# Two forward passes of a four-layer attention kernel: scores in halves, sums in the score banks, one ring of PSUM banks, and a planner that looks further ahead

## The chip, the core and the metric

The kernel runs on one core of one Trainium2 chip. The metric is the device time of one execution in microseconds, median of several runs. The core's engines work side by side, each through its own list of instructions in order: TensorE (PE, matmuls, results into PSUM), VectorE (DVE), ScalarE (ACT), GpSimd (POOL) and SyncE (SP, which here issues nearly all DMAs). PSUM is eight banks of 512 floats in each of 128 partitions.

## The reference

Four residual layers over x (2048 tokens, 640 features, 32 heads of 20), A, B, A, B, with the same weights for both A and for both B; then the gradients of all five inputs for a given `grad_out`. The output is x after four layers and the gradients.

```python
# layer A: linear attention; phi(t) = where(t > 0, t + 1, exp(t)) + 1e-6
pq, pk = phi(q), phi(k)
kv = jnp.einsum("bhsd,bhse->bhde", pk, v)     # sums over all tokens
z = jnp.einsum("bhsd->bhd", pk)
o = jnp.einsum("bhqd,bhde->bhqe", pq, kv) / (jnp.einsum("bhqd,bhd->bhq", pq, z)[..., None] + 1e-6)

# layer B: causal attention over a window of 256 tokens
scores = jnp.einsum("bhqd,bhkd->bhqk", q, k) * (Dh ** -0.5)
p = _softmax(jnp.where(mask[None, None], scores, -1e9), axis=-1)
o = jnp.einsum("bhqk,bhkd->bhqd", p, v)

x = x + _A_ref(_layernorm(x), A_wqkv, A_wo)
x = x + _B_ref(_layernorm(x), B_wqkv, B_wo)   # and both once more
```

Layer A needs the sums kv and z over all tokens before its first output; layer B needs only the tile before and the two tiles ahead of it. That shapes the staging.

## The kernel before

Tokens are worked in 16 tiles of 128. `forward` has three stages. The first computes layer 0's q, k, v and its sums tile by tile (`a_first`, `kv_tile`). Then `ab_pass(0, False)` goes through the tiles once: the output of layer 0 (`a_num`, `out_proj`), layernorm, layer 1's qkv (`b_qkv`), its attention (`attn`), its output projection, and, one to three tiles behind, layer 2's layernorm, k and v (`a_first(items, l + 2, ...)`). `a_kv(2)` then forms layer 2's sums from all tiles, and `ab_pass(2, True)` does layers 2 and 3 and prepares what the backward part starts with (`dO`, `early`). `bwd_phase` follows; neither its functions nor its own planner's settings differ between the two kernels.

The order on every engine is made ahead of time. Each step calls `op(engine, duration, function, reads, writes)`; the items of a pass are sorted by a due time in tiles, and `Sched.order` places the operations one by one, with the assumed durations, on the engine that can start earliest. Among PE's operations it takes only those whose rank in the list is less than `ahead` (AHEAD = 12) past the first one not yet placed. `emit` writes the instructions in that order, and on the chip each engine follows it, waiting on semaphores. An operation on PE that waits therefore holds up all behind it.

PSUM in the passes: `R["mm"]` is a ring of three banks (`free=True`: the planner gives an operation the bank that comes free first) for all projections, transposes through PE and a_num; `R["s"]` is one tile of four banks for the scores; `R["pv"]` is one bank for the attention's values. Together eight.

The attention of a tile has eight groups of four heads. For a group, `scores` issues 4 matmuls for each key tile, 12 from the third tile on (L734: each uses 32 of PE's 128 rows, at row offset 32 x head, and head `hh` writes bank `hh` of the score tile), then one exp on ACT over all four banks (L739), and the masks: `affine_select` on POOL (L743, twice) and, for three key tiles, one multiply on DVE (L748) and one more select on POOL (L751). `values` multiplies the exps with v in two halves of two heads (L768); 16 heads share a values bank, which is then emptied by a reciprocal and a multiply on DVE (L775, L776). The multiply writes the tile `oB`; in the second pass oB lies in the memory of the tile `kv`, and the trace calls it kv there. The exps lie in a ring of three tiles `e_sb`.

`a_kv` sums with one bank of the ring for each of five bands of features: 16 matmuls each over the tiles (L571), and a sixth bank for z: 80 matmuls of one column (L583). DVE multiplies each band with a mask into `mbd` (L590, `masked`), as soon as that band is summed, and spreads z into `zsel` (L595, L597, `store_mbd`); SP stores `mbd`. `kv_tile`, used in the first stage alone, instead adds one tile's ten matmuls (five bands, five columns of z) to two banks `sums` that stay open for all tiles. `a_num` reads mbd (L647 numerators; the 32-column matmuls of L480 with zsel are the denominators). A projection is a chunk of 320 columns: five matmuls at L480, emptied by one operation of DVE or ACT.

Of the kernel before, what the change touches and what calls it, by code (L numbers as in the profile page):

```python
# [23 lines left out]
QL = 3  # L24
QS = 0.5


# [59 lines left out]
class Sched:  # L87

    def __init__(self, tc, ahead=None, lead=None):
        self.tc, self.ops, self.lw, self.rd, self.ahead, self.lead = tc, [], {}, {}, ahead, lead

# [32 lines left out]
    def order(self):  # L126
# [42 lines left out]
        while len(out) < len(self.ops):  # L169
# [35 lines left out]
            o.start = t  # L205
# [24 lines left out]
class Kern:  # L230
# [130 lines left out]
    def forward(self):  # L361
# [7 lines left out]
        with ExitStack() as st:  # L369
# [90 lines left out]
            def vp(n):  # L460
                return 150 + 1.04 * n
# [101 lines left out]

            def a_kv(l):
                def band_sum(m, lo, hi):
                    w_ = hi - lo
                    ps = R["mm"].buf()
                    for t0 in range(0, TT, 4):
                        def f(t0=t0):
                            for tt in range(t0, t0 + 4):  # L570
                                nc.tensor.matmul(ps.t[:, 0:w_], lhsT=pk(tt, m * P, (m + 1) * P), rhs=vv(tt, lo, hi),  # L571
                                                 start=(tt == 0), stop=(tt == TT - 1))
                        op("PE", pe([w_] * 4), f, [k for tt in range(t0, t0 + 4) for k in
                                                   (("pk", tt, 2), ("pk", tt, 3), ("vv", tt, 4), ("vv", tt, 5))], [ps])
                    masked(m, ps, 0)

                for m in range(DT):
                    band_sum(m, *self.band[m])
                zp = R["mm"].buf()
                for m in range(DT):  # L580
                    def f(m=m):
                        for tt in range(TT):
                            nc.tensor.matmul(zp.t[:, m:m + 1], lhsT=pk(tt, m * P, (m + 1) * P),  # L583
                                             rhs=self.ones_bf[:, 0:1], start=(tt == 0), stop=(tt == TT - 1))
                    op("PE", pe([1] * TT), f, [("pk", tt, i) for tt in range(TT) for i in (2, 3)], [zp])
                store_mbd(l, zp, 0)

            def masked(m, ps, off):
                lo, hi = self.band[m]
                op("DVE", vp(hi - lo), lambda: nc.vector.tensor_mul(  # L590
                    mbd[:, m, lo:hi], ps.t[:, off:off + hi - lo], self.bmask[:, m, 0:hi - lo]), [ps, "masks", "zeros"],
                   [("mbd", m)])

            def store_mbd(l, zp, off):
                op("DVE", vp(DT), lambda: nc.vector.tensor_copy(zcol, zp.t[:, off:off + DT]), [zp], ["zcol"])  # L595
                for m in range(DT):
                    op("DVE", v2(H), lambda m=m: nc.vector.tensor_scalar(  # L597
                        out=zsel[:, m, :], in0=self.hmask[:, m, :], scalar1=zcol[:, m:m + 1], scalar2=None,
                        op0=ALU.mult), ["zcol", "masks", "zeros"], [("zsel", m)])
                dma("SP", lambda: self.sv[l]["mbd"].rearrange("(m p) e -> p m e", p=P), lambda: mbd, 960 * KB,  # L600
                    [(k, m) for m in range(DT) for k in ("mbd", "zsel")], [])

            def kv_tile(tt, sums):

                def f():
                    for m, (lo, hi) in enumerate(self.band):
                        i, off = at_[m]
                        lhsT = pk(tt, m * P, (m + 1) * P)
                        nc.tensor.matmul(sums[i].t[:, off:off + hi - lo], lhsT=lhsT, rhs=vv(tt, lo, hi),
                                         start=(tt == 0 and m == 0), stop=(tt == TT - 1), skip_group_check=True)  # L610
                        nc.tensor.matmul(sums[1].t[:, zoff + m:zoff + m + 1], lhsT=lhsT, rhs=self.ones_bf[:, 0:1],
                                         start=(tt == 0 and m == 0), stop=(tt == TT - 1), skip_group_check=True)
# [102 lines left out]
            def attn(l, b, qT, kTs, vts, oT, out):  # L715
# [10 lines left out]
                def scores(g):  # L726
                    def f():
                        s = R["s"].buf()

                        def mm_s():  # L730
                            for j in range(nkt):
                                for hh in range(4):
                                    r = slice(HPAD * hh, HPAD * (hh + 1))
                                    nc.tensor.matmul(s.t[:, hh, j * P:(j + 1) * P], lhsT=kTs[j].t[r, g, :],  # L734
                                                     rhs=qT.t[r, g, :], start=True, stop=True,
                                                     tile_position=(HPAD * hh, 0))
                        op("PE", 210 + 55 * nkt, mm_s, [qT] + kTs, [s])
                        e = es[g] = R["e"].buf()
                        op("ACT", av(4 * nkt * P), lambda: nc.scalar.activation(  # L739
                            e.t[:, :, 0:nkt, :], s.t[:, :, 0:nkt * P].rearrange("p h (i q) -> p h i q", q=P),  # L740
                            ACT.Exp, scale=self.c_att), [s], [(e, p_, j) for p_ in (0, 1) for j in range(nkt)])
                        for p_ in (0, 1):
# [13 lines left out]
                def values(g, p_):  # L756
                    def f():
                        e = es[g]
                        q = 4 * g // 16
                        if q not in pvs:  # L760
                            pvs[q] = R["pv"].buf()
                        pv = pvs[q]

                        def mm_pv():
                            for hh in (2 * p_, 2 * p_ + 1):
                                h = 4 * g + hh
                                for j in range(nkt):
                                    nc.tensor.matmul(pv.t[:, h % 16, :], lhsT=e.t[:, hh, j, :],  # L768
                                                     rhs=vts[j].t[:, h, :], start=(j == 0), stop=(j == nkt - 1))
                        op("PE", pe([DH + 1] * 2 * nkt), mm_pv,  # L770
                           [(e, p_, j) for j in range(nkt)] + [(v, c) for v in vts for c in (4, 5)], [pv])
                        if g % 4 == 3 and p_ == 1:
                            h0 = 16 * q
                            li = lambda: lv.t[:, i_, h0:h0 + 16]
                            op("DVE", 200, lambda: nc.vector.reciprocal(li(), pv.t[:, :, DH]), [pv], [(lv, i_, q)])  # L775
                            op("DVE", vp(16 * DH), lambda: nc.vector.tensor_tensor(  # L776
                                out=o.t[:, h0 * DH:(h0 + 16) * DH].rearrange("p (h d) -> p h d", d=DH),
                                in0=pv.t[:, :, 0:DH], in1=li().unsqueeze(2).to_broadcast([P, 16, DH]), op=ALU.mult),
                               [pv, (lv, i_, q)], [(o, q)] + ok)
# [145 lines left out]
            def ab_pass(l, last):  # L925
# [81 lines left out]
                else:  # L1007
                    a_first(items, l + 2, 2.09, -0.2)
                run(items)

# [9 lines left out]
            sums_p = pool1("sums_ps", **PS)  # L1020
            sums = [Ring(1, tiles=[sums_p.tile([P, 512], F32, name=f"sums{i}")], name="sums").buf() for i in range(2)]
            items = []
# [8 lines left out]
            run(items)  # L1031
            for m in range(DT):
                masked(m, sums[at_[m][0]], at_[m][1])
            store_mbd(0, sums[1], zoff)
            S.emit()
# [753 lines left out]
```

## Time and profile before

| what | value |
|---|---|
| median of three runs | 2114.66 us (2114.49 to 2114.9) |
| the profiled execution: its own time | 2109.33 us |
| its span, first to last instruction | 2107.4 us |
| granted TensorE clock, mean | 0.984 |
| first A layer | 0 to 76 us |
| first pass | 76 to about 400 us, last exp of scores ends at 387.26 |
| second pass | 407 to 706 us, last exp of scores ends at 700.5 |
| backward part | 706 to 2107 us |

How to read it: the page gives busy time of each engine as a share of the span, and the costliest groups of instructions with line, engine, operation, tiles and shapes. A window row gives, for each engine, busy us and (instructions), then the granted clock (1.00 is full), the share of the DMA engines and GB/s. A timeline row is start, duration, engine, line, operation, tiles, shapes, count; in brackets is the engine's idle time just before and what ended it. A row of waits is: who waited, for whose result, us in total, how many times, the longest. Durations of matmuls include a modelled tail, so two in a row overlap in the rows; start to start tells their cost.

### The profile page before, as it was taken

The page shows a single profiled execution, that of the slowest core. Times are in us where ns is not written, and L with a number is a line of the kernel's source. Part 1 is how long each engine was busy: PE and PEld are TensorE (multiplying, and loading weights), DVE is VectorE, ACT ScalarE, POOL GpSimd, SP SyncE. Part 2 cuts the span into 40 slices and gives each one's busy share as a digit, 9 for nine tenths or more (in the row PEclk, how much of TensorE's full clock was granted, in tenths as well). Part 3 has the DMA queues.
Part 4 walks back from the last instruction along what each step waited for, and adds up shares of the span by engine and source line. Part 5 has one row for each costly group of instructions (what it writes and reads, how often), then busy time and mean ns, then how long its engine had stood idle before and what let it go on. Part 6 is the DMA issues. An engine that isn't in the chain of part 4 may idle for free. (4 is left out here: it accounts for less than half of the span.)

```text
span 2107.4 us, 68065 instructions
## 1 busy us (share of the span) xinstructions
PE 1982.7 (94%) x28001; PEld 1362.9 (65%) x28001; DVE 1437.3 (68%) x2978; ACT 1169.3 (55%) x1946; POOL 840.8 (40%) x1851
## 2 busy tenths in 40 slices
PE   7889999799898899999999999999999999999999
PEld 5656555566555577777665677656777776666764
DVE  8767776567776799999143369606999994444641
ACT  5367888358777688887222223215888872211330
POOL 1044555236666666665022213203666652221210
PEclk9999999899999899999999999998999999999999
DMA  8689877379998699997999999738889879899973
GB/s 309 196 189 216 180 180 184 109 175 195 211 202 191 129 151 165 159 156 122 190 200 191 256 209 207 181 97 159 139 144 144 147 122 183 190 204 241 212 172 90
DMA packets 926568, 373.72 MB, mean 177 GB/s; under 512 B 816944, under 2 KB 902960, under 8 KB 926000
## 3 DMA queue, kind: packets, MB, share of 16 engines
q1 hardware_dynamic: 885616, 337.77, 79.3%
q10 hardware_dynamic: 40640, 31.60, 5.2%
q8 instruction: 219, 3.59, 0.7%
q14 instruction: 93, 0.76, 0.1%
HBM read 106.73 MB, written 112.23 MB: 104 GB/s over the span
## 5 line engine op out<-in xcount | busy, mean ns | idle before, releaser
L1606 DVE SCALAR_TENSOR_TENSOR ds_sb<-pair,e_sb 128x768 bf16<-128x768 f32 x480 | 439.4, 952 | 18.8 <-POOL e_sb L1595 6.8
L1591 ACT ACTIVATE e_sb<-pair 128x768 bf16<-128x768 f32 x480 | 379.1, 812 | 96.1 <-PE pair L1571 94.8
L739 ACT ACTIVATE e_sb<-s_ps 128x1536 bf16<-128x1536 f32 (+2 forms) x256 | 350.6, 1370 | 98.7 <-PE s_ps L734 56.6
L743 POOL TENSOR_SCALAR_AFFINE_SELECT e_sb<-e_sb 128x256 bf16<-128x256 bf16 x512 | 213.2, 439 | 378.2 <-ACT e_sb L739 361.0
L1098 PEld LDWEIGHTS <-om 128*128 128x128 bf16 x1920 | 188.3, 98 | 157.0 <-DMA om<-o 2.2
L1098 PE MATMUL mm_ps<-wq,dqT 128*128 128x320 bf16 x1920 | 276.0, 299 | 4.7 <-ACT dqkv L1430 3.7
L1259 POOL TENSOR_TENSOR gw<-w,gcar 128x640 f32<-128x640 f32 x64 | 89.9, 1405 | 456.7 <-ACT w L1256 451.2
L1098 PE MATMUL mm_ps<-dqkv,om 128*128 128x480 bf16 x1280 | 268.9, 367 | 1.4 <-DMA om<-hn 1.4
L1598 POOL TENSOR_SCALAR_AFFINE_SELECT e_sb<-e_sb 128x256 bf16<-128x256 bf16 x448 | 182.1, 406 | 199.9 <-ACT e_sb L1591 199.9
L1595 POOL TENSOR_SCALAR_AFFINE_SELECT e_sb<-e_sb 128x256 bf16<-128x256 bf16 x512 | 206.5, 407 | 78.5 <-ACT e_sb L1591 78.5
L1098 PEld LDWEIGHTS <-dqT 128*128 128x128 bf16 x1920 | 185.9, 98 | 79.0 <-issue 6.6
L1241 ACT ACTIVATE dh<-mm_ps 128x320 f32<-128x320 f32 x128 | 56.0, 437 | 292.0 <-PE mm_ps L1098 234.3
L1624 PE MATMUL dsT_ps<-ident,ds_sb 128*128 128x128 bf16 x2244 | 189.5, 221 | 3.8 <-DVE dsT L1627 1.3
L480 PE MATMUL mm_ps<-Wqkv_B,hnTB 128*128 128x320 bf16 x960 | 180.4, 300 | 10.7 <-DMA hnTB<-hnB 6.5
L768 PEld LDWEIGHTS <-e_sb 128*128 128x128 bf16 x2880 | 122.2, 97 | 74.7 <-POOL e_sb L751 20.0
L768 PE MATMUL pv_ps<-v_slab,e_sb 128*128 128x32 bf16 x2880 | 145.0, 178 | 19.0 <-DVE oB L776 4.6
L1627 DVE COPY dsT<-dsT_ps 128x768 bf16<-128x768 bf16 x268 | 147.8, 552 | 7.7 <-PE dsT_ps L1624 4.7
L480 PE MATMUL mm_ps<-Wqkv_A,pqT 128*128 128x320 bf16 x780 | 139.2, 302 | 5.8 <-DVE oA L657 2.4
L1571 PE MATMUL pair<-VTg,dOTg 32*128 32x384 bf16 (+2 forms) x896 | 139.9, 318 | 1.0 <-ACT e_sb L1591 0.3
L1624 PEld LDWEIGHTS <-ds_sb 128*128 128x128 bf16 x2244 | 132.4, 98 | 12.1 <-issue 9.3
L1645 PE MATMUL dqvk_ps<-Qsl,ds_sb 128*128 128x32 bf16 x2880 | 134.7, 177 | 3.2 <-ACT dqkv L1627 2.7
L1261 DVE SCALAR_TENSOR_TENSOR gcar<-hn,sm,gw 128x640 bf16<-128x640 bf16 x64 | 80.4, 1256 | 82.0 <-POOL gw L1259 82.0
(178 smaller groups left out, 3556.5 us busy)
## 6 DMA issues: line engine op xcount, KB each, us to landing
qkvp<-qk_slab SPq DMA_DIRECT2D x32, 512.0 KB, 3.1
om<-o SPq DMA_DIRECT2D x20, 512.0 KB, 5.9
hn<-hn SPq DMA_DIRECT2D x64, 160.0 KB, 3.0
om<-hn SPq DMA_DIRECT2D x20, 512.0 KB, 4.9
ee<-e SPq DMA_DIRECT2D x32, 320.0 KB, 3.7
e<-ee SPq DMA_DIRECT2D x52, 160.0 KB, 2.0
qkvp<-v_slab SPq DMA_DIRECT2D x32, 256.0 KB, 2.7
o<-o SPq DMA_DIRECT2D x48, 160.0 KB, 3.4
```

The costliest lines, as they stand in the source:

```text
L480: nc.tensor.matmul(ps.t[:, w0:w0 + width], lhsT=lhsT(), rhs=rhs(), start=start, stop=stop)
L739: op("ACT", av(4 * nkt * P), lambda: nc.scalar.activation(e.t[:, :, 0:nkt, :], s.t[:, :, 0:nkt * P].rearrange("p h (i q) -> p h i q", q=P) ...
L743: op("POOL", 440, lambda p_=p_: nc.gpsimd.affine_select(out=e.t[:, 2 * p_:2 * p_ + 2, nkt - 1, :], in_=e.t[:, 2 * p_:2 * p_ + 2, nkt - 1, ...
L768: nc.tensor.matmul(pv.t[:, h % 16, :], lhsT=e.t[:, hh, j, :], rhs=vts[j].t[:, h, :], start=(j == 0), stop=(j == nkt - 1))
L1098: nc.tensor.matmul(ps.t[:, w0:w0 + width], lhsT=lhsT(), rhs=rhs(), start=start, stop=stop)
L1571: nc.tensor.matmul(ps[:, i, c0:c0 + len(ks) * P], lhsT=ld[g][lhs][r, q * P:(q + 1) * P], rhs=ld[g][rhs][r, ks[0] * P:(ks[-1] + 1) * P], st ...
L1591: nc.scalar.activation(e, PR[h][:, :, 0:3 * P].rearrange("p i (j q) -> p i j q", q=P), ACT.Exp, scale=self.c_att)
L1595: nc.gpsimd.affine_select(out=e[:, :, j, :], in_=e[:, :, j, :], compare_op=ALU.is_ge, fill=0.0, base=0, pattern=[[0, 2], [-1, P]], channel ...
L1598: nc.gpsimd.affine_select(out=e[:, :, j, :], in_=e[:, :, j, :], compare_op=ALU.is_ge, fill=0.0, base=-1, pattern=[[0, 2], [1, P]], channel ...
L1606: nc.vector.scalar_tensor_tensor(out=DS[n][:, hs], in0=PR[h][:, :, 0:3 * P].rearrange("p i (j q) -> p i j q", q=P), scalar=self.c_att, in1 ...
L1624: nc.tensor.transpose(ps[:, i, j, :], DS[n][:, 2 * p + i, j, :], self.ident)
L1627: (nc.vector.tensor_copy if eng == "DVE" else nc.scalar.copy)(out, in_)
```

## The change

Four parts, all in `forward` and in the planner:

- The scores of the last 12 groups of each pass (tile 14 from group 4 on, and tile 15) are done in two halves of two heads: six matmuls and one exp over two banks each, with keys of their own, `("s_ps", 0)` and `("s_ps", 1)`. All other groups stay whole. The planner's duration for a half's matmuls is that of a whole group.
- `a_kv` and `masked` go. In the first pass 16 operations `kv_tile` add layer 2's sums to banks 2 and 3 of the score tile; the first takes them over after the last scores' exp. `store_mbd` does the five masked products, then z.
- The three `mm` banks and the values bank become one ring of four, and a tile's values take a bank of it.
- In the planner of the passes an operation of ACT, DVE or POOL frees its engine 100, 80 or 50 ns ahead of its result, and PE's window is 16 operations instead of 12. The first stage keeps 12 and no such lead.

```diff
+TAIL = dict(PE=0, ACT=100, DVE=80, POOL=50)
...
-                free[e] = t + o.dur
-                o.end = free[e] + (170 if e == "PE" else 0)
+                free[e] = t + o.dur - (self.tail[e] if self.tail else 0)
+                o.end = t + o.dur + (170 if e == "PE" else 0)
...
-            def a_kv(l):
-                def band_sum(m, lo, hi):
...
-            def masked(m, ps, off):
...
+            def store_mbd(l, sums, keys=()):
+                for m, (lo, hi) in enumerate(self.band):
+                    i, off = at_[m]
+                    op("DVE", vp(hi - lo), lambda m=m, lo=lo, hi=hi, i=i, off=off: nc.vector.tensor_mul(
+                        mbd[:, m, lo:hi], sums[i][:, off:off + hi - lo], self.bmask[:, m, 0:hi - lo]),
+                       ["sums", "masks", "zeros"] + list(keys), [("mbd", m)])
+                op("DVE", vp(DT), lambda: nc.vector.tensor_copy(zcol, sums[1][:, zoff:zoff + DT]), ["sums"] + list(keys), ["zcol"])
...
-            def kv_tile(tt, sums):
+            def kv_tile(tt, sums, keys=None):
...
-                   [("pk", tt, 2), ("pk", tt, 3), ("vv", tt, 4), ("vv", tt, 5)], sums)
+                   [("pk", tt, 2), ("pk", tt, 3), ("vv", tt, 4), ("vv", tt, 5)], ["sums"] if tt else ["sums"] + (keys or []))
...
                 def scores(g):
                     def f():
-                        s = R["s"].buf()
...
-                        op("PE", 210 + 55 * nkt, mm_s, [qT] + kTs, [s])
                         e = es[g] = R["e"].buf()
-                        op("ACT", av(4 * nkt * P), lambda: nc.scalar.activation(
-                            e.t[:, :, 0:nkt, :], s.t[:, :, 0:nkt * P].rearrange("p h (i q) -> p h i q", q=P),
-                            ACT.Exp, scale=self.c_att), [s], [(e, p_, j) for p_ in (0, 1) for j in range(nkt)])
+                        for h0, h1 in ((0, 2), (2, 4)) if 2 * b * G + 2 * g >= (2 * TT - 3) * G else ((0, 4),):
+                            halves = range(h0 // 2, h1 // 2)
+
+                            def mm_s(h0=h0, h1=h1):
+                                for j in range(nkt):
+                                    for hh in range(h0, h1):
...
+                            op("PE", 210 + 55 * nkt, mm_s, [qT] + kTs, [("s_ps", p_) for p_ in halves])
+                            op("ACT", av((h1 - h0) * nkt * P), exp, [("s_ps", p_) for p_ in halves],
+                               [(e, p_, j) for p_ in halves for j in range(nkt)])
...
-                            pvs[q] = R["pv"].buf()
+                            pvs[q] = R["mm"].buf()
...
                     a_first(items, l + 2, 2.09, -0.2)
+                    for tt in range(TT):
+                        items.append((max(16.1 + 0.15 * tt, tt + 3.9), len(items), lambda tt=tt: kv_tile(
+                            tt, [s_ps[:, i, :] for i in (2, 3)], [("s_ps", 1)])))
...
-            S = Sched(tc, ahead=AHEAD)
-            R["mm"] = banks(pool("mm_ps", **PS), 3, "mm_ps")
-            R["s"] = Ring(1, tiles=[pool("s_ps", **PS).tile([P, 4, 512], F32, name="s_ps")])
-            R["pv"] = ring("pv_ps", 1, [P, 16, 32], F32, **PS)
+            S = Sched(tc, ahead=16, tail=TAIL)
+            R["mm"] = banks(pool("mm_ps", **PS), 4, "mm_ps")
+            s_ps = pool("s_ps", **PS).tile([P, 4, 512], F32, name="s_ps")
             ab_pass(0, False)
-            a_kv(2)
+            store_mbd(2, [s_ps[:, i, :] for i in (2, 3)], [("s_ps", 1)])
             ab_pass(2, True)
```

More of the change, by code (lines that the diff above doesn't have):

```diff
@@ L87, with __init__ @@
 class Sched:
-    def __init__(self, tc, ahead=None, lead=None):
-        self.tc, self.ops, self.lw, self.rd, self.ahead, self.lead = tc, [], {}, {}, ahead, lead
+    def __init__(self, tc, ahead=None, lead=None, tail=None):
+        self.tc, self.ops, self.lw, self.rd, self.ahead, self.lead, self.tail = tc, [], {}, {}, ahead, lead, tail
     def op(self, eng, dur, fn, r=(), w=(), dma=None, prio=None):
@@ L562, in a_qkv @@
                 return [chunk(ci) for ci in cis]
-            def a_kv(l):
-                def band_sum(m, lo, hi):
[L566 to L586, printed above, removed]
@@ L588, in masked @@
-            def masked(m, ps, off):
[L589 to L595, printed above, removed]
+            def store_mbd(l, sums, keys=()):
[5 more added lines that the diff above has]
+                op("DVE", vp(DT), lambda: nc.vector.tensor_copy(zcol, sums[1][:, zoff:zoff + DT]), ["sums"] + list(keys), ["zcol"])
@@ L727, in f @@
                     def f():
-                        s = R["s"].buf()
[L730 to L736, printed above, removed]
@@ L737, in f, with exp @@
-                        op("PE", 210 + 55 * nkt, mm_s, [qT] + kTs, [s])
-                        e = es[g] = R["e"].buf()
-                        op("ACT", av(4 * nkt * P), lambda: nc.scalar.activation(
-                            e.t[:, :, 0:nkt, :], s.t[:, :, 0:nkt * P].rearrange("p h (i q) -> p h i q", q=P),
-                            ACT.Exp, scale=self.c_att), [s], [(e, p_, j) for p_ in (0, 1) for j in range(nkt)])
+                        e = es[g] = R["e"].buf()
+                        for h0, h1 in ((0, 2), (2, 4)) if 2 * b * G + 2 * g >= (2 * TT - 3) * G else ((0, 4),):
[3 more added lines that the diff above has]
+                                    for hh in range(h0, h1):
+                                        r = slice(HPAD * hh, HPAD * (hh + 1))
+                                        nc.tensor.matmul(s_ps[:, hh, j * P:(j + 1) * P], lhsT=kTs[j].t[r, g, :],
+                                                         rhs=qT.t[r, g, :], start=True, stop=True,
+                                                         tile_position=(HPAD * hh, 0))
+                            def exp(h0=h0, h1=h1):
+                                nc.scalar.activation(
+                                    e.t[:, h0:h1, 0:nkt, :],
+                                    s_ps[:, h0:h1, 0:nkt * P].rearrange("p h (i q) -> p h i q", q=P),
+                                    ACT.Exp, scale=self.c_att)
+                            op("PE", 210 + 55 * nkt, mm_s, [qT] + kTs, [("s_ps", p_) for p_ in halves])
+                            op("ACT", av((h1 - h0) * nkt * P), exp, [("s_ps", p_) for p_ in halves],
+                               [(e, p_, j) for p_ in halves for j in range(nkt)])
@@ L767, in mm_pv @@
                                 for j in range(nkt):
-                                    nc.tensor.matmul(pv.t[:, h % 16, :], lhsT=e.t[:, hh, j, :],
+                                    nc.tensor.matmul(pv_h()[:, h % 16, :], lhsT=e.t[:, hh, j, :],
                                                      rhs=vts[j].t[:, h, :], start=(j == 0), stop=(j == nkt - 1))
@@ L774, in f @@
                             li = lambda: lv.t[:, i_, h0:h0 + 16]
[L775 removed]
+                            op("DVE", 200, lambda: nc.vector.reciprocal(li(), pv_h()[:, :, DH]), [pv], [(lv, i_, q)])
                             op("DVE", vp(16 * DH), lambda: nc.vector.tensor_tensor(
                                 out=o.t[:, h0 * DH:(h0 + 16) * DH].rearrange("p (h d) -> p h d", d=DH),
[L778 removed]
+                                in0=pv_h()[:, :, 0:DH], in1=li().unsqueeze(2).to_broadcast([P, 16, DH]), op=ALU.mult),
                                [pv, (lv, i_, q)], [(o, q)] + ok)
@@ L1020, in forward @@
             sums_p = pool1("sums_ps", **PS)
-            sums = [Ring(1, tiles=[sums_p.tile([P, 512], F32, name=f"sums{i}")], name="sums").buf() for i in range(2)]
+            sums = [sums_p.tile([P, 512], F32, name=f"sums{i}") for i in range(2)]
             items = []
@@ L1031, in forward @@
             run(items)
-            for m in range(DT):
-                masked(m, sums[at_[m][0]], at_[m][1])
-            store_mbd(0, sums[1], zoff)
+            store_mbd(0, sums)
             S.emit()
```

5 lines of the change are left out of this document (3 added, 2 removed).

## The prediction, made before the changed kernel had run

> **What bounds the kernel now.** First the page's header and its table of busy times, for the total and the fullest engine:
>
> ```profile
> span 2107.4 us, 68065 instructions
> PE 1982.7 (94%) x28001; PEld 1362.9 (65%) x28001; DVE 1437.3 (68%) x2978; ACT 1169.3 (55%) x1946; POOL 840.8 (40%) x1851
> ```
>
> PE is the bound, but an average over 2107 us hides where it idles. So next the busy times in windows cut at the stages: start, ramp of the first pass, its steady part, its last 12 groups of scores, the turn to the second pass, the same again, then the backward part.
>
> ```profile
> core 0: us, PE busy (x) PEld busy (x) DVE busy (x) ACT busy (x) POOL busy (x), PEclk, DMA share, GB/s
> 100.00:362.00 262.00, 242.00 (x3831) 154.83 (x3830) 189.47 (x527) 203.46 (x275) 132.61 (x329) 1.00 0.83 191
> 362.00:387.30 25.30, 20.97 (x358) 13.93 (x357) 13.62 (x39) 19.65 (x21) 14.64 (x36) 0.87 0.30 96
> 387.30:430.00 42.70, 32.84 (x363) 23.58 (x362) 25.81 (x73) 6.43 (x19) 1.17 (x3) 0.88 0.50 145
> 430.00:676.50 246.50, 226.35 (x3723) 147.09 (x3723) 179.97 (x482) 186.79 (x215) 149.40 (x342) 1.00 0.92 194
> 676.50:706.30 29.80, 22.43 (x378) 14.92 (x377) 16.66 (x41) 17.69 (x13) 18.78 (x42) 0.89 0.44 115
> ```
>
> The change can only move these 606 us and the ramp ahead of them (76 to 100): PE's instruction lists of the two kernels agree before row 1259 and after row 18782, that is, in the first A layer and in all of the backward part (1401 us, PE 97% busy). PE idles 20 us in each steady part, 4.3 and 7.4 in the two tails, 9.9 in the turn. What ends those idles is in the waits of PE over 76 to 706 us:
>
> ```profile
> PE s_ps L734 <- ACT e_sb L739: 9.0, 26, 0.7
> PE pv_ps L768 <- DVE oB L776: 4.6, 10, 0.8
> PE mm_ps L480 <- DVE pp L548: 4.3, 16, 0.8
> PE pv_ps L768 <- DVE kv L776: 4.1, 5, 0.9
> PE mm_ps L480 <- DVE oA L657: 2.4, 8, 0.4
> PE mm_ps L480 <- DVE qk_slab L699: 2.3, 7, 0.3
> PE mm_ps L480 <- DVE gcar L548: 1.1, 1, 1.1
> ```
>
> (us in total, times, longest.) The first is the score banks, not yet emptied by the exp. The two L776 rows are the one values bank, not yet emptied by the multiply into oB (8.7 us). In the others PE waits on DVE for tiles that none of these matmuls reads directly (pp reaches PE only through a DMA): a bank of the ring of three (10.1 us, and single rows of 0.6).
>
> **Halves.** The timeline of the first tail shows the loop:
>
> ```profile
> 370.31 0.35 PE L734 MATMUL s_ps<-QT,KT 32*128 32x128 bf16 x12 [0.71 <-ACT e_sb L739]
> 370.59 0.58 PE L480 MATMUL mm_ps<-Wqkv_A,pqT 128*128 128x320 bf16 x3
> 370.75 1.45 ACT L739 ACTIVATE e_sb<-s_ps 128x1536 bf16<-128x1536 f32 x1 [0.50 <-POOL e_sb L743]
> 372.25 0.35 PE L734 MATMUL s_ps<-QT,KT 32*128 32x128 bf16 x12 [0.39 <-ACT e_sb L739]
> ```
>
> Scores, 0.35; hand-over, 0.09; exp, 1.45; hand-over, 0.05: 1.94 us from score to score, and nothing shortens it while one tile of four banks is written and read as a whole. The last 12 groups take 25.2 us in pass one (362.02 to the end of the exp at 387.26) and 24.0 in pass two (676.53 to 700.5). In halves, PE fills two banks while ACT reads the other two. ACT's cost: one more instruction per group. The backward part has an exp of just that size, 768 columns:
>
> ```profile
> 721.43 1.51 ACT L1591 ACTIVATE e_sb<-pair 128x768 bf16<-128x768 f32 x2 [0.22 <-PE pair L1571]
> ```
>
> Two in a row take 1.51, against 1.45 for the whole: 0.06 a group. ACT's floor is then 12 x 1.51 = 18.1 us, plus in pass one the other ACT work among these groups (six of 0.42, one rs pair of 0.49: 3.0). So at best -4.1 (25.2 to 21.1) and -5.9 (24.0 to 18.1). PE's cost: row 370.59 follows 0.28 after the scores begin, so a group occupies PE for 0.28: twelve matmuls of 128 columns in the time of five transposes of 128 columns (396.10 to 396.39), because its four heads lie in four row groups and run side by side. A half has two side by side, and costs between half of the 0.28 (no loss) and all of it (+0.28 a group, 3.3 us a pass). By a four-matmul group (429.76, the next matmul at 429.93: 0.17) most is fixed cost, so I take the whole +0.28. Pass one then has 21.0 + 3.3 = 24.3 of PE work in 25.2, part of it at half clock (its row 378.68 takes 0.98 for what row 370.59 did in 0.58). I take -2.0 a pass, -4.0. Worst: if PE sets the pace and nothing hides the second half, +3.3 a pass. Masks keep pace: POOL has about 1.28 a group (two of 0.44, one of 0.40).
>
> The Trainium skill, TensorEngine Tiling (Array Packing), Tiling Modes, says that a change of tiling mode drains TensorE, which speaks against twice as many score blocks. The 0.17 for four matmuls against 0.28 for twelve, 0.014 each, leaves some 0.115 a block, which agrees; by that rule 24 more blocks cost 2.8 us of PE, and if none were hidden the -4.0 would be -1.2.
>
> **Sums in the score banks.** Removed: a_kv's sums, after the pass.
>
> ```profile
> 400.68 0.65 PE L571 MATMUL mm_ps<-gcar 128*128 128x140 bf16 x8
> 406.95 0.42 PE L647 MATMUL mm_ps<-mbd,pqT 128*128 128x320 bf16 x3
> 407.62 0.73 PE L480 MATMUL mm_ps<-mbd,pqT 128*128 128x32 bf16 x5 [0.25 <-DVE mbd L597]
> 75.44 1.17 DVE L590 TENSOR_TENSOR mbd<-sums,bmask 128x140 bf16<-128x140 f32 x5 [0.39 <-PE sums L609]
> ```
>
> They fill PE from 400.68 to 406.95 (12 of the matmuls came earlier, at 396.39), and the first denominator starts at 407.62. Added: the same 160 matmuls as 16 tiles of ten, 0.44 us each (first A layer: 27.24 to 27.68). In the new list two tiles stand right after the last scores, 13 more among what was there, the sixteenth just ahead of the second pass. PE's idles from the last exp (387.26) to 400.68 are 0.79 + 0.44 + 0.45 + 1.36 + 0.65 = 3.7; 0.75 more comes free at 396.39. Fifteen tiles are 6.6: 2.2 overflow onto the path. That path is long and serial (last values, oB, out-projection, layernorm, qkv of the last tile). The last v copy ends at 401.37; then 0.05, the sixteenth tile 0.44, then DVE's five masked products, zcol and zsel, which no longer lie beside the sums: in the first layer the first denominator (77.00) starts 1.6 after the last sum. 401.37 + 0.5 + 1.6 + 2.2 = 405.7 against 407.62: -1.9. Ends: -4.1 (no overflow), +2.5 (all 6.6 on the path). The first tile waits for the last exp with all of PE's queue behind it; next there are the last values, which wait for that exp and then 0.8 of POOL's masks, so the wait is free; uncovered, the two tiles cost 0.9. The store of mbd stays one DMA on SP, behind the same products. The second pass's scores wait for the products to leave these banks, some 20 us before they are due.
>
> **One ring of four.** Along the two instruction lists, with 0.136 us a 320-column matmul (20 in 2.71 at 69.85) and 0.026 a values matmul, I counted the PE work between two uses of a bank: under 0.9 us 23 times before and 11 after, under 1.2 us 70 and 27; after a values block it is never under 1.1. Emptying a values bank took 1.2 (block ends 380.52, next at 381.73). So the 8.7 us should go, and half of the 10.1. Of these 13.8 I let half arrive: in the steady parts scores follow each other by 2.0 to 2.2, against the loop's 1.94, and PE is 92% busy. -6.9; ends -13.8 and 0. At the start of pass two both out-projection chunks shared a bank (414.07 waits 0.58 for x L676); now they have two: -0.6.
>
> **Planner.** Tails and 16 instead of 12 add no instruction; they reorder. The other waits on DMA (hnTB 6.5, oTA 4.5) and on masks (e_sb 4.4 + 3.8 + 1.3) are 20 us; a third either way is 7. I take 0. Clock: 0.87 to 0.89 over 98 us is about 23 us at half speed, in which matmuls took 1.7 times as long; up to 9.6 us if PE-bound throughout. I take no change.
>
> Sum: -4.0 - 1.9 - 6.9 - 0.6 = -13.4. The profiled execution took 2109.3 (span and 1.9 around it): 2095.9. The runs' median is 2114.7, 5.3 above; there the forecast is **2101.3**.
>
> **Rivals.**
> - *The clock holds.* The half-clock stretches lie in the tails and the turn, where PE stops and starts. If shorter stops keep it full, half of the 9.6 comes on top: 2096.5. For: 0.98 against 0.58 above. Against: the turn's long serial path stays, and its stretch from 409 followed waits on DVE that remain. The Trainium skill, TensorE: Matmul & The Clock Gate, on psum-queue cycling, says that micro-idles between groups make the clock oscillate. By it, fewer bank waits would raise PEclk; the steady parts, at 1.00 with the same waits, do not bear it out.
> - *Waits move on.* A bank comes free, and PE then stands for masks, DMA or the score loop. Only halves and sums count, at half: 2111.7. For: steady spacing is within 0.2 of the loop. Against: every tile has a gap of 2.4 to 2.9 too.
> - *Values starve the chunks: slower.* Values now draw on the common ring; at each of 64 hand-overs two values banks are held, and chunks have two. A chunk is 0.68 of PE, its emptying about 0.65 and 0.1 of hand-over twice; each hand-over then stalls PE by up to 0.3: 19 us, less 4.0 + 1.9 + 0.6: 2127, or 2121 if a third is hidden. It decides once chunks return to a bank within about 0.9 us as a rule; the count (11 times) speaks against it.
> - *It does not do what it says:* halves give nothing, PE paying twice. That is the forecast without 4.0: 2105.3, inside its range.
>
> **Chances.** Forecast 0.55 (own range 2094 to 2108); clock holds 0.10; waits move on 0.20; starving 0.15. Within 0.2% (2110.4 to 2118.9), about what a measurement of this kernel can tell from no change, lies most of the third and a little of the fourth: 0.14. Slower 0.15, faster 0.71. The range takes in the third and the clock, and leaves out most of the fourth: 2091 to 2117.
>
> **What would show it.** Right: the L776 rows on pv gone from PE's waits; last 12 scores of each pass in about 23 and 22 us; first denominator of pass two some 18.5 us after the last exp (20.4 now); PE over 93% busy in steady parts. Wrong: new rows of mm_ps waiting for DVE; score spacing unchanged; POOL or DMA ahead of values in PE's waits; PEclk lower.

## The result, and the profile after

The kernel became slower: 2130.21 us, median of four runs (2127.32 to 2131.94), against 2114.57 for the kernel before in the same session. The two medians divide to 1.0074; the ratio on record, used from here on, is 1.0064, 95% interval 1.0048 to 1.0079. The forecast was 2101.3, its range 2091 to 2117, with 0.15 on slower.

The profiled execution took 2129.36 us, 0.9 under its median, and that of before 2109.33, 5.3 under: differences between these two profiles come out some 4 us too large. The first lines of its page, span and the busy times of PE:

```profile
span 2127.6 us, 68070 instructions
PE 2003.2 (94%) x28001; PEld 1369.2 (64%) x28001; DVE 1434.3 (67%) x2978; ACT 1172.3 (55%) x1970; POOL 840.3 (39%) x1851
```

PE has the same 28001 matmuls and is busy 20.5 us longer (2003.2 against 1982.7): the same work, part of it at a lower clock. The stages tell where. Windows of after, cut as before at the first scores of a pass, the first halves, the last exp, and so on:

```profile
core 0: us, PE busy (x) PEld busy (x) DVE busy (x) ACT busy (x) POOL busy (x), PEclk, DMA share, GB/s
97.70:360.20 262.50, 242.38 (x3816) 153.81 (x3814) 185.52 (x522) 202.34 (x273) 133.57 (x330) 0.99 0.84 191
360.20:394.10 33.90, 28.15 (x329) 16.13 (x330) 11.80 (x34) 20.38 (x31) 15.49 (x37) 0.58 0.20 67
394.10:439.00 44.90, 38.74 (x404) 28.31 (x401) 28.78 (x80) 7.80 (x23) 0.76 (x2) 0.82 0.50 145
439.00:684.40 245.40, 226.84 (x3717) 144.68 (x3715) 179.23 (x479) 186.50 (x213) 147.04 (x343) 1.00 0.87 195
684.40:718.00 33.60, 25.69 (x328) 15.15 (x327) 11.04 (x29) 19.11 (x24) 16.72 (x39) 0.59 0.32 87
```

The two tails, which the halves were to shorten, take 33.9 and 33.6 us at a clock of 0.58 and 0.59. Half clock, 69 us in all before, is now 115 us. As times of the n-th group's exp (the starts, and in brackets the difference to before):

| exp of group | before | after | e1 whole scores | e9 halves in own tiles |
|---|---|---|---|---|
| 0, first of pass one | 102.9 | 97.7 (-5.2) | 100.2 (-2.7) | 97.9 (-4.9) |
| 116, first of the last 12 | 362.5 | 360.3 (-2.2) | 364.0 (+1.5) | 361.2 (-1.3) |
| 127, last of pass one | 385.8 | 391.9 (+6.1) | 385.5 (-0.3) | 379.6 (-6.3) |
| 144, steady part of pass two | 461.6 | 466.8 (+5.2) | 457.1 (-4.5) | 451.6 (-10.1) |
| 244, first of the last 12 | 677.0 | 684.4 (+7.4) | 678.2 (+1.2) | 671.5 (-5.4) |
| 255, last of pass two | 699.1 | 716.1 (+17.0) | 700.8 (+1.6) | 688.8 (-10.3) |
| first exp of the backward part | 706.7 | 724.1 (+17.4) | 709.9 (+3.2) | 696.8 (-9.9) |

The column of after loses 8.3 us between groups 116 and 127, 9.6 between 244 and 255, and 17.4 stand when the backward part begins. From the first exp of group 116 to the end of 127's the tail was 24.8 us and is 33.8; in pass two 23.6 became 33.2. The timeline of after in the second tail, with the rows of other work left out, shows the loop:

```profile
687.25 0.50 PE L714 MATMUL s_ps<-QT,KT 32*128 32x128 bf16 x6 [0.57 <-ACT e_sb L719]
...
687.79 0.81 ACT L719 ACTIVATE e_sb<-s_ps 128x768 bf16<-128x768 f32 x1 [0.59 <-PE s_ps L714]
...
688.65 0.50 PE L714 MATMUL s_ps<-QT,KT 32*128 32x128 bf16 x6 [0.62 <-ACT e_sb L719]
...
689.24 0.81 ACT L719 ACTIVATE e_sb<-s_ps 128x768 bf16<-128x768 f32 x1 [0.64 <-PE s_ps L714]
...
690.10 0.50 PE L714 MATMUL s_ps<-QT,KT 32*128 32x128 bf16 x6 [0.52 <-ACT e_sb L719]
```

Each L714 row is one half's scores, each L719 row one half's exp. The exp at 687.79 ends at 688.60, and the other half's scores start at 688.65: they wait for it, though it reads other banks. Then ACT waits 0.64 for them. PE and ACT take turns: no scores are written while an exp of scores runs. Two halves, one group, take 2.85 us here (687.25 to 690.10), where a whole group took 1.94. The program itself says why: both halves lie in one tile, s_ps, and the semaphore count that each block of scores waits for is that of the exp issued last, of whichever half. The keys `("s_ps", 0)` and `("s_ps", 1)` separate the halves for the planner; the waits are made per tile.

PE's waits over the passes (76 to 726 us), the four largest, and the same for the second tail alone (684 to 718), where there is one row only:

```profile
PE s_ps L714 <- ACT e_sb L719: 20.0, 54, 1.0
PE mm_ps L483 <- DMA hnTB<-hnB: 10.4, 8, 2.3
PE mm_ps L753 <- DVE e_sb L732: 8.0, 19, 0.6
PE mm_ps L483 <- DMA oTA<-oA: 4.3, 6, 1.0
```

```profile
PE s_ps L714 <- ACT e_sb L719: 8.2, 16, 0.9
```

Waits on score banks went from 9.0 to 20.0 us; 13.5 of them lie in the two tails. The rows of the values bank (8.7 us) are gone, as forecast. But other rows grew: hnTB 6.5 to 10.4, masks of DVE 4.4 to 8.0. In the steady parts PE is 92% busy, as before, and not over 93%, the sign that the prediction had named.

### The profile page after: what moved, and what is told of

It is laid out like the page before. It is cut to its first block, busy times and chain, and to the rows that moved or that the text cites. A ratio compares the mean times of both kernels' runs of the same rounds, so it can differ in the third digit from the quotient of the medians.

```text
span 2127.6 us, 68070 instructions
## 1 busy us (share of the span) xinstructions
PE 2003.2 (94%) x28001; PEld 1369.2 (64%) x28001; DVE 1434.3 (67%) x2978; ACT 1172.3 (55%) x1970; POOL 840.3 (39%) x1851
## 5 line engine op out<-in xcount | busy, mean ns | idle before, releaser
L1591 DVE SCALAR_TENSOR_TENSOR ds_sb<-pair,e_sb 128x768 bf16<-128x768 f32 x480 | 439.2, 952 | 19.2 <-POOL e_sb L1580 6.5
L719 ACT ACTIVATE e_sb<-s_ps 128x1536 bf16<-128x1536 f32 (+3 forms) x280 | 353.8, 1267 | 115.5 <-PE s_ps L714 74.3
L483 PE MATMUL mm_ps<-Wqkv_B,hnTB 128*128 128x320 bf16 x960 | 181.3, 303 | 12.2 <-DMA hnTB<-hnB 10.4
L753 PEld LDWEIGHTS <-e_sb 128*128 128x128 bf16 x2880 | 126.6, 97 | 77.1 <-POOL e_sb L735 22.7
L753 PE MATMUL mm_ps<-v_slab,e_sb 128*128 128x32 bf16 x2880 | 152.4, 179 | 10.3 <-DVE e_sb L732 8.0
```

The source lines that it names most:

```text
L483: nc.tensor.matmul(ps.t[:, w0:w0 + width], lhsT=lhsT(), rhs=rhs(), start=start, stop=stop)
L719: nc.scalar.activation(e.t[:, h0:h1, 0:nkt, :], s_ps[:, h0:h1, 0:nkt * P].rearrange("p h (i q) -> p h i q", q=P), ACT.Exp, scale=self.c_att)
L753: nc.tensor.matmul(pv_h()[:, h % 16, :], lhsT=e.t[:, hh, j, :], rhs=vts[j].t[:, h, :], start=(j == 0), stop=(j == nkt - 1))
L1591: nc.vector.scalar_tensor_tensor(out=DS[n][:, hs], in0=PR[h][:, :, 0:3 * P].rearrange("p i (j q) -> p i j q", q=P), scalar=self.c_att, in1 ...
```

## The experiments

Twelve kernels, four at a time, each four beside the kernel before on one chip. That kernel's median was 2121.6, 2123.4 and 2121.0 us in those sessions, so only the ratios are compared.

| kernel | ratio to before | 95% interval | tails, us |
|---|---|---|---|
| before | | | 24.8, 23.6 |
| after | 1.0064 | 1.0048 to 1.0079 | 33.8, 33.2 |
| e1 after, whole scores | 0.9979 | 0.9958 to 0.9999 | 22.9, 24.0 |
| e2 before, with halves | 1.0085 | 1.0068 to 1.0101 | 31.6, 34.4 |
| e3 two tiles for all groups | 0.9960 | 0.9943 to 0.9977 | 20.0, 18.6 |
| e4 whole scores, exps in halves | 1.0016 | 1.0002 to 1.0031 | 26.1, 28.7 |
| e5 e1 with the old planner | 0.9958 | 0.9941 to 0.9974 | 23.5, 24.8 |
| e6 e1 with its own values bank | 0.9983 | 0.9971 to 0.9995 | 23.7, 24.9 |
| e7 e3 with whole blocks | 1.0037 | 1.0022 to 1.0053 | 26.2, 29.0 |
| e8 e3 with the old planner | 0.9992 | 0.9978 to 1.0006 | 21.0, 20.4 |
| e9 after, own tiles in the tails | 0.9940 | 0.9916 to 0.9964 | 19.9, 18.8 |
| e10 before, halves in own tiles | 0.9983 | 0.9970 to 0.9996 | 20.6, 20.1 |
| e11 e9 with the old planner | 0.9938 | 0.9919 to 0.9957 | 20.5, 19.1 |
| e12 e9 with its own values bank | 0.9961 | 0.9946 to 0.9976 | 19.6, 21.3 |

**e1_whole** and **e2_before_halves** divide the change: everything but the halves, and the halves alone.

```diff
-for h0, h1 in ((0, 2), (2, 4)) if 2 * b * G + 2 * g >= (2 * TT - 3) * G else ((0, 4),):
+for h0, h1 in ((0, 4),):
```

(e1, in after; e2 puts after's function `scores` with one tile s_ps into before and nothing else.)

> The changed kernel with all score groups whole again (no halves); sums in the score banks, ring of four and planner stay. Theory A (serial halves: both halves lie in one tile, and each half's scores wait for the exp issued last, of either half, so a group is two loops of 0.05 + 0.34 + 0.09 + 0.81 = 1.3 us at full clock where a whole group is one of 1.94): the two tails lose 33.8 to 25.2 and 33.2 to 24.0 us again, 18 us, so about 2112 us. Theory B (clock: score blocks that fill half of PE's rows pull the clock to half, and that is the loss): also about 2112, it cannot be told from A here. Theory C (the ring, the sums or the planner lost the time): 2125 or more.

> The kernel before with the halves alone. A and B: each tail grows by some 8 to 10 us, 2132 us. C: 2115, as before.

Without the halves the change is 0.9979; alone, the halves cost 0.0085, and going from e1 to after costs the same 0.0085, 18 us. So within the intervals the loss is all in the halves, and it doesn't depend on ring, sums or planner.

**e3_two_tiles** and **e4_half_exps** ask what about the halves costs it. In e3 the score banks are two tiles of two banks for all groups (a tile is read by one exp, so every group has two); only the last 12 have their matmuls in halves too. e4 keeps after's one tile and twelve matmuls in one block, and halves the exps of the last 12 groups alone.

```diff
-s_ps = pool("s_ps", **PS).tile([P, 4, 512], F32, name="s_ps")
+s_pool = pool("s_ps", **PS)
+s_h = [s_pool.tile([P, 2, 512], F32, name=f"s_half{i}") for i in range(2)]
```

> The changed kernel with the score banks as two tiles of two banks: the last 12 groups in halves as in the change, the others with twelve matmuls in a row and two exps. A: a half now waits for its own exp alone; the last 12 groups take 25 us or less in pass one and 24 or less in pass two, half clock in all about 70 us as before the change, total 2112 or less. B: half blocks still pull the clock to half, tails stay over 30 us, total about 2128.

> The changed kernel, one tile, with the last 12 groups' twelve matmuls whole and only the exp in two. A: one loop a group of 0.05 + 0.35 + 0.09 + 1.51 = 2.0 us, so tails as with whole groups plus 0.7 us each, 2113 us. B: whole blocks keep the clock, 2113 too; half clock in all about 70 us. C: 2128.

e3 has tails of 20.0 and 18.6 us and no half clock in them. e4 was to cost 1.4 us over e1 and cost 0.0037, about 8. Its timeline in the second tail shows a wait that I hadn't thought of:

```profile
688.81 0.28 DVE L733 TENSOR_TENSOR e_sb<-e_sb,maskT_first 128x256 bf16<-128x256 bf16 x1
...
689.15 0.34 PE L754 MATMUL mm_ps<-v_slab,e_sb 128*128 128x32 bf16 x6 [0.62 <-DVE e_sb L733]
...
689.42 0.51 PE L713 MATMUL s_ps<-QT,KT 32*128 32x128 bf16 x12
...
690.12 1.51 ACT L721 ACTIVATE e_sb<-s_ps 128x768 bf16<-128x768 f32 x2 [1.50 <-PE s_ps L713]
```

The scores (L713) stand in PE's list behind a values block (L754) that waits for a mask of DVE (L733), and ACT idles 1.50 us for scores whose banks had been free for 0.8 us when PE came to them (the exps before end at 688.62). In this tail PE waits 4.9 us for that mask; in e1's it is 0.9.

**e5 to e8** undo single parts of e1 and e3: the planner's lead and window (e5 on e1, e8 on e3: `Sched(tc, ahead=12)`), the ring of four (e6 on e1: values in a bank `pv`, three banks in `mm`), and the split of the matmuls (e7 on e3: `tail_ = False`).

> After's ring of four and sums in the score banks, all scores whole, but the planner of the passes as it was: window 12, no lead. It is e1_whole with one part undone. In e1_whole (ratio 0.9979) the steady parts gave back what the ramps had gained: from group 16 to 115 of pass one 5.6 us against before, from group 16 to 115 of pass two 5.7. Theory P (the planner's lead or window costs this): both steady parts lose less than 1 us against before, and the kernel comes out 6 to 10 us under e1_whole, ratio about 0.994. Theory R (the ring of four costs it): they still lose 5 to 6 each and the ratio stays at 0.998. Theory W (waits only move on, each list of operations has its own sum of them): steady parts anywhere within 5 us of before, ratio 0.996 to 1.002, with the waits on hnTB or on masks taking the place of those on banks.

> e1_whole with the values back in a bank of their own and three in the ring; the new planner stays. Theory P: steady parts still lose 5 to 6 us each against before, ratio 0.998 or above. Theory R: they lose less than 1 us, ratio about 0.994. The prediction's term for the ring (waits on the values bank 8.7 us, half of 10.1 on the others) would have it slower than e1_whole by 7 us: ratio 1.001. Theory W: within 5 us of e1_whole either way, with the rows of PE waiting for oB and kv on the values bank back at some 8 us in total.

> e3_two_tiles (ratio 0.9960) with its last 12 groups done like the others: one block of twelve matmuls and two exps, so the matmuls must wait for both tiles. If e3's short tails come from PE filling one half while ACT reads the other, the 12 last groups of each pass go back from about 20 to about 24.5 us, and the kernel is 7 us slower than e3 where the tails are not covered: ratio 0.999. If they come from the two exps alone (masks start a half earlier), tails stay at 20 to 21 us and the ratio at 0.996.

> e3_two_tiles with the planner of the passes as it was (window 12, no lead). Theory P: 6 to 10 us under e3_two_tiles, ratio about 0.992, steady parts no slower than before's. Theory R: within 2 us of e3_two_tiles, ratio 0.995 to 0.997. The tails stay at about 20 us by both, since they hang on the two tiles.

e7 is clear: with whole blocks the two tiles lose what they gave, 0.0077 or 16 us, and the tails go to 26.2 and 29.0, further than the 24.5 I had expected. There, as in e4, PE waits for masks of DVE in front of values (5.8 us in the second tail). With e9 below this makes a square, though in e3 and e7 all the other groups have two exps as well. Two exps and one block of scores cost time with one tile (e4) and with two (e7); splitting the scores too makes it worse with one tile (after) and pays only with two (e3, e9).

e5, e6 and e8 give the planner no sign of its own: the old planner is 0.0021 better on e1, with overlapping intervals, and 0.0032 worse on e3. The ring of four is 0.0004 better than the values' own bank on e1, inside the intervals. But e6 does not bring back the waits that the ring was to remove. Before has 8.7 us of waits on the values bank, theory W expected some 8, and e6 has 2.1 in the passes:

```profile
PE pv_ps L753 <- DVE oB L761: 2.1, 1, 2.1
```

So the order of e6, made by the new planner, avoids most of these waits without the ring, and e6 cannot price the ring for the old planner. The time from group 16 to 115 of the passes, 225.8 and 213.4 us before, is 231.4 and 219.1 in e1, 227.2 and 215.5 in e5, 228.3 and 215.8 in e6: longer in all three. This is no measure of ring or planner, though: e10 below has the same lists as before on every engine in these two stretches, and takes 229.2 and 216.9. Theory R misses the ratios of e5, e6 and e8, and theory P wanted 0.992 for e8 and got 0.9992. W, that each list has its own sum of waits, is what is left; its ranges are wide, and it is not shown in detail.

**e9_after_own_tiles** is the test that changes the waits and nothing else. The score banks are taken anew at each turn from whole groups to halves and back; the instructions and their order on every engine are those of after, apart from the instructions that only wait.

```diff
+class Scores:
+    def tiles(self, n):
+        if self.n != n:
+            if self.st:
+                self.st.close()
+            self.n, self.st = n, ExitStack()
+            p_ = self.make(self.st)
+            self.t = [p_.tile([P, 4 // n, 512], F32, name="s_ps" if n == 1 else f"s_half{i}") for i in range(n)]
+        return self.t
...
 def mm_s(h0=h0, h1=h1):
+    k = h1 - h0
+    ts = s_ps.tiles(4 // k)
...
-nc.tensor.matmul(s_ps[:, hh, j * P:(j + 1) * P], lhsT=kTs[j].t[r, g, :],
+nc.tensor.matmul(ts[hh // k][:, hh % k, j * P:(j + 1) * P], lhsT=kTs[j].t[r, g, :],
```

**e10** does the same to e2, and **e11** and **e12** put e9 on the old planner and on the values' own bank.

> After, with the same instructions in the same order on every engine. Only the score banks are taken anew at each turn: one tile of four banks while groups are whole, two tiles of two banks (s_half0, s_half1) for the last 12 groups of a pass, so that a half's scores wait for the exp of their own half two back, and not for the exp issued last. After itself gave 1.0064. Theory T (one tile is what makes the halves wait for each other): the last 12 groups of the passes fall from 33.8 and 33.2 us to about 20, most of the half clock in them goes, and the kernel comes to about 0.995, 20 to 25 us under after. Theory C (two small score blocks cost PE more, and its stops take the clock; the tile has nothing to do with it): tails 30 us or more, ratio 1.004 or above. Theory M (the wait goes but another takes its place): tails 24 to 27, ratio 0.998 to 1.000, with masks or DMA ahead of values in PE's waits.

> Before, with halves alone (no sums in score banks, no ring of four, old planner), and the halves in two tiles as in e9_after_own_tiles. It is e2_before_halves (1.0085) with the tile split. It measures the prediction's term for the halves by itself: -4.0 us, best -10.0, so a ratio of 0.998, best 0.9953; last 12 groups in about 23 and 22 us, or 21 and 18 at best. Theory T: 0.995 to 0.998. Theory C: 1.005 or above. Theory M: 0.999 to 1.002.

> e9_after_own_tiles with the planner of the passes as it was (window 12, no lead). With whole scores the old planner was 0.0021 under the new one (0.9958 against 0.9979), with two tiles for all groups it was 0.0032 over it (0.9992 against 0.9960). If the planner has an effect of its own, this comes out 4 us or more under e9. If its effect is chance of each list (theory W), anything within 0.003 of e9 either way.

> e9_after_own_tiles with the values in a bank of their own and three banks in the ring. The prediction's term for the ring has this 7.5 us slower than e9 (+0.0035). With whole scores, e6_whole_pv_bank against e1_whole, it was 0.0004. If the ring of four gives nothing, this is within 0.001 of e9.

e9 is 0.9940: 1.2% or 26 us under after, by the tile alone. Theories C and M fall as accounts of the loss. The windows of its two tails:

```profile
361.20:381.10 19.90, 19.75 (x336) 12.24 (x335) 11.20 (x34) 19.24 (x31) 15.25 (x37) 1.00 0.33 114
...
671.50:690.40 18.90, 18.23 (x326) 11.51 (x327) 10.47 (x29) 17.83 (x24) 16.36 (x39) 1.00 0.59 155
```

PE is busy 19.75 of 19.90 us and ACT 19.24, where after had 28.15 and 20.38 of 33.90; the clock is 1.00 instead of 0.58. The timeline at the start of the second tail (eight exps in one row), and what PE waits for there:

```profile
671.54 6.03 ACT L749 ACTIVATE e_sb<-s_half 128x768 bf16<-128x768 f32 x8 [0.48 <-PE s_half L744]
...
672.67 0.34 PE L744 MATMUL s_half<-QT,KT 32*128 32x128 bf16 x6
...
672.94 0.45 PE L511 MATMUL mm_ps<-Wo_B,oTB 128*128 128x320 bf16 x2
...
673.32 0.34 PE L744 MATMUL s_half<-QT,KT 32*128 32x128 bf16 x6
...
673.96 0.34 PE L744 MATMUL s_half<-QT,KT 32*128 32x128 bf16 x6
...
674.75 0.34 PE L744 MATMUL s_half<-QT,KT 32*128 32x128 bf16 x6
```

```profile
PE s_half L744 <- ACT e_sb L749: 0.5, 1, 0.5
```

ACT runs eight exps without a gap, 0.75 each, while PE writes the halves ahead of them. PE's wait on the score banks in this tail is 0.5 us, once, for 8.2 us in 16 waits in after.

e10, the halves alone but in own tiles, is 0.9983 or -3.6 us (interval -6.3 to -0.8), the expected -4.0. Its tails are 4.2 and 3.5 us shorter than those of before, where -2.0 each was expected, so that the total agrees partly by luck: 3.4 and 3.5 us are gone again in the steady parts, in which every engine has before's instructions in before's order. That is how far single profiles of the same work, taken in different sessions, lie apart here. e11 is level with e9. e12 is 0.0021 over e9 where the prediction's term wanted 0.0035, and the intervals overlap: not resolved. Eight of the twelve have an interval wholly below 1 (e1, e3, e5, e6, e9 to e12); e9 and e11 lie lowest.

## Why the prediction was wrong

**Halves: -4.0 predicted, and this is the step that failed.** It says: "In halves, PE fills two banks while ACT reads the other two." That took the planner's two keys for two tiles. The diff shows one tile s_ps in both kernels, and the prediction itself had said of the kernel before that nothing shortens the loop "while one tile of four banks is written and read as a whole". Measured, the halves cost 18 us as built (e1 to after, 0.0085), and bring 8 us in own tiles (e1 to e9, 0.0039). From -4.0 to +18 is 22 of the 27 us between forecast (-13.4) and result (0.0064, +13.5); e1, which has the other terms alone, accounts for the rest with -4.4 us (interval -8.9 to -0.2) against -9.4. The PE side was right: the prediction took the whole +0.28 a group, and a half holds PE as long as a whole group does (0.27, from 672.67 to 672.94 in e9). In own tiles this is hidden behind ACT's exps, and the worst case of +3.3 a pass did not come: from the first scores the tails of e9 take 20.3 and 19.1, beside best cases of 21.1 and 18.1.

**The rival "it does not do what it says" was the true one, at the wrong price.** It had halves that give nothing cost only the lost 4.0: 2105.3. But two loops in a row are no loop of the old length. By rows: 0.34 for a half's matmuls as for a whole group's, hand-overs of 0.09 and 0.05, and 0.81 for an exp of 768 columns that stands alone, so 1.29 a half at full clock and 2.58 a group against 1.94; 24 groups are +15.4, and the forecast without the 4.0 becomes 2120.7. After's rows at half clock, 2.85 a group, add 0.27 each, 6.5 in all: 2127.2, against 2130.2 measured. That this comes so close is partly luck: it prices the halves at 21.9, where 18 was measured, and still counts on -9.4 from the other terms, of which e1 shows -4.4.

**Clock: "I take no change".** It fell because of the waits: e9 has the same list and 57 us of half clock where after has 115. Of the signs of being wrong, a lower PEclk was seen, and the score spacing, named as unchanged, even grew.

**Sums in score banks: -1.9, with the first denominator 18.5 us after the last exp.** It is 20.7 in after, where the last exps are late and slow, and 19.2 in e1 and e9, from 20.4 before: -1.2. In e10, which keeps the old sums and has short tails, it is 22.0: -2.8 by that. The term was about right. The row in e9, whose last exp ends at 381.1:

```profile
400.31 0.72 PE L511 MATMUL mm_ps<-mbd,pqT 128*128 128x32 bf16 x5
```

**One ring of four: -6.9.** The rows of L776 are gone, but what that was worth stays open. PE's waits of e9 over the passes show what stands first now:

```profile
PE mm_ps L511 <- DMA hnTB<-hnB: 13.7, 11, 2.4
PE mm_ps L783 <- DVE e_sb L762: 7.7, 18, 0.6
PE s_ps L744 <- ACT e_sb L749: 6.7, 29, 0.5
```

hnTB was 6.5 before and the masks 4.4; the 6.7 us on the score banks lie outside the tails, where before has 3.8. So in the changed kernel waits did move on, as a rival had it. That the ring makes PE wait longer on hnTB is not shown: with the ring and the old planner (e11) it is 7.0. The steady parts from group 16 to 115 took 225.8 and 213.4 us before, 228.9 and 215.6 in after, 229.7 and 218.1 in e9: 3.1 and 2.2 more, 3.9 and 4.7 more, where before's own lists take 3.4 and 3.5 more in e10. By ratios, on the new planner the ring gives 0.0004 (e6) and 0.0021 (e12), neither clear of nothing; there the values' own bank has only 2.1 and 1.7 us of waits left. On the old planner sums and ring together (e5) give -8.9 us, interval -12.5 to -5.5, where the prediction had -9.4; no run has the ring alone on it. The rival of starved chunks did not come: after's waits have no row on the ring's emptying among the largest.

**Planner: 0, with 7 either way.** The old planner against the new one is -0.0021 on e1, +0.0032 on e3 and -0.0002 on e9: no sign of its own, and the bound of 7 us held.

The sum, -13.4, is close to what e9 measures (-0.0060, -12.7) and e11 (-0.0062, -13.1), each with some 4 to 5 us either way. Part of that is chance: in e9 the halves gave twice their term and the rest half of theirs. Also, profiles differ in places that no edit touches: from the 211th to the 241st exp of the backward part 480.1 us pass in before and after, 483.3 in e9, 484.4 in e10, with the same instructions.

## What to carry to other kernels

Overlap between two parts of a buffer needs two things: an order that allows it, and waits that are kept apart for the parts. Look in the built program which count a block waits for, before believing in keys of a planner. A rival that says "the overlap does not come" must be priced as the serial loop, hand-overs included and at the clock that such a loop gets, and not as the lost gain. And a wait that vanishes from an engine's list is worth only what the rows behind it leave: compare times between the same two instructions, not sums of waits, and first see how far these times differ where the lists are the same (3 to 4 us in some 220 here).

## What the runs showed of the hardware

TensorE fell to half clock in a stretch of short stops. Half clock began 5.6 us after the first halves and lasted 30.7 us without a break. In those 5.6 us PE was busy 3.64 us and stood three times for the score banks, 1.9 us in all; in the whole first tail it was busy 28.15 of 33.90 us, most of it already at half clock, and stood ten times, 5.3 us in all and never over 1.0. With the same instructions in the same order and these stops gone, it stayed at full clock through both tails (e9). This agrees with the rule of the Trainium skill, TensorE: Matmul & The Clock Gate, on psum-queue cycling, that micro-idles between groups of matmuls make the clock swing, though here it stayed low and did not swing. The prediction had set the rule aside because the steady parts held 1.00 "with the same waits". There they are rare: 4 and 8 on the score banks in the two steady parts before, of 260 and 246 us, against 10 and 16 in after's two tails of 34 us each. How many stops it takes is not shown: before's second tail has 14 in 23.5 us (8 on the score banks), and only 6.8 us of half clock.

Splitting a block of twelve small matmuls into two of six doubles its cost on PE. From its first matmul to the next one of other work, a block of twelve holds PE for 0.28 us, and one of six for 0.27 (the median of 41 at full clock in e9). Blocks of four and eight, over one and two key tiles, take 0.17 and 0.22, so in these runs the time goes by the key tiles, three for a half as for a whole group, and not by the number of matmuls (the prediction had read 0.014 for each). A group pays 0.27 more, 3.2 us a pass, and e9 hides it. The drain between tiling modes, from TensorEngine Tiling (Array Packing), Key Properties, in the Trainium skill, was priced at 2.8 us for the 24 blocks in the prediction; no run here parts a drain from the rest of a block's 0.27.
